# A fused attention and feed-forward kernel: the load of w_in in quarters of whole rows, batch 1's k behind it, and new orders of work for all five engines

## The chip, the cores and the metric

The kernel runs on 1 core of one Trainium2 chip. Its time is the device time of one execution in microseconds (us), as the median of several executions. The profile is of one execution, whose own time is given beside its span (the time from its first to its last instruction).

## The reference

Two stages follow one another. The first is block attention with a sorting matrix: `sort_net` (4 batches x 8 heads, each 8x8) goes through five rounds of exp and of division by row sums and by column sums (the sinkhorn steps); the result P mixes the 8 blocks of k and of v, and each block of 96 queries attends to its own mixed block of 96 keys.

```python
B, H, S, D = 4, 8, 768, 64          # 8 blocks of 96
for _ in range(5):
    P = exp(P - max(P, -1)); P = P / sum(P, -1); P = P / sum(P, -2)
k_sorted = einsum('bhij,bhjcd->bhicd', P, k_b)      # v_sorted alike
attn = softmax(q_b @ k_sb.T / 8)                    # per batch, head and block
x = (attn @ v_sb) as 3072 tokens x 512
h = x @ w_in                                        # w_in 512 x 2048
g = max(h, 0) + alpha * min(h, 0)
out = g @ w_out                                     # w_out 2048 x 512
```

## The kernel before

All work is cut into 1227 numbered operations (`G.add`, numbered in the order in which they are added). An operation is a small group of instructions on one engine or one DMA. The program does not run in the order of the numbers: the table `SEQ` lists all the numbers in one global order, and each engine takes its own operations in that order, strictly one after the other. A letter behind a number (p, a, d) chooses POOL, ACT or DVE where an operation may run on more than one engine. The waits between engines follow from what the operations read and write (`_Graph.emit`). So a table can move an operation ahead of or behind others on its engine, or to another engine, and an operation that waits holds up all that stands behind it in its engine's list. `WARM` adds matmuls on the identity whose result nobody reads (fillers, line 808): `114:9:y` puts nine of them into PE's list ahead of operation 114. `BURST` is the number of still smaller matmuls at the very start (line 888).

The attention works on groups g = 0 to 31, eight per batch. For each group: scores (line 715 in batch 0, line 712 later), their maximum on DVE (line 721), in batch 0 a second set of scores with the maximum subtracted (lines 736 and 727), exp on ACT, the product with v (line 768), the division on DVE (lines 776 and 779), and a transpose into xT (line 794 on PE, or a DMA). In batches 1 to 3 the exponentials, and q itself, are transposed by DMAs from SP's queue (ET at line 753, QTz at line 409).

Before attention, k and v of each batch are mixed: in batch 0 by matmuls at lines 600 (k) and 674 (v) after a conversion of v on POOL or DVE (line 653); later by conversions at lines 616 (k) and 658 (v), and matmuls at lines 629 and 669, with the results copied out at line 372. In batch 0 the k result also needs a pad copy (line 642) before any scores.

The feed-forward part takes tokens in chunks: the first matmul of w_in per tile of 128 features (`ffn1`, line 823), two steps on ACT (line 833) and DVE (line 836) that make hT, then `ffn2` (line 862) in four parts per 128 tokens; parts 0 and 1 read the first half of w_out, parts 2 and 3 the second.

The loads from HBM are issued by POOL into one queue (the software queue): q, k and v of batch 0 first (lines 397 and 419), then in some order k of batch 1 (419), w_in in four quarters (907), w_out in two halves (912), v of batch 1 in two halves (435) and q of batch 1 in eight pieces, one per head (401). They change f32 to bf16 on the way; the sizes in the profile are those of the bf16 result.

The operations that the texts below name by number: 4, 5, 6 the loads of q, k, v of batch 0; 130 to 133 the quarters of w_in; 134 and 135 the halves of w_out; 138 the load of k of batch 1; 147 and 148 v of batch 1; 139 to 146 q of batch 1; 403, 402 and 404 the first halves of v and the k of batch 2; 10 the memset of sel0; 72 the exp of the fifth sinkhorn round; 97 the pad copy; 158 the first scores; 196 and 193 the first two operations of ffn1; 273 the first part of the first ffn2; 361 an ffn1, 373 an ffn2 part, 383 a product with v, 388 a mixing of v; 191, 229, 235 and 238 a transpose, two ffn1 and one scores operation of batch 0; 250 a conversion of k of batch 1; 178 to 183 the transposes of q of batch 1 (QTz), of which 178 is the first; 419 the scores of group 8, the first of batch 1, which read the result of 178; 422 the ET transpose of group 8.

## Time and profile before

| | us |
|---|---|
| three executions | 238.43, 238.87, 239.08 |
| their median | 238.87 |
| the profiled execution's own time | 238.79 |
| its span | 237.1 |

| engine | busy us | share of the span | instructions |
|---|---|---|---|
| PE (matmul) | 228.4 | 96% | 2511 |
| DVE | 169.4 | 71% | 353 |
| ACT | 151.9 | 64% | 423 |
| POOL | 74.1 | 31% | 140 |

The granted TensorE clock has a mean of 1.000. The profile gives for each instruction its engine, its line in the kernel, its tiles and what it waited for. A matmul's record lasts longer than its turn on the engine, since matmuls overlap; the chain of waits shows the turns. The table of windows gives each engine's busy time in a stretch of the span, the share of the DMA engines' time taken by packets (over 1 where packets overlap) and the bytes moved.

### The profile page before, as it was taken

Reading aid. Unit: us, or ns where it says so; the run is one execution under the profiler, and the core shown is the slowest. Engines: PE = TensorE matmul, PEld = TensorE weight load, DVE = VectorE, ACT = ScalarE, POOL = GpSimd, SP = SyncE. Lnnn points to the kernel's source line nnn. Section 1 sums busy time; section 2 is a strip of 40 time slices with the busy share of each in tenths; the row PEclk is TensorE's granted clock in tenths of the full one; section 3 lists DMA queues with packets and bytes.
Section 4 is the critical chain, followed back from the end, with each engine's and each line's share of the span. In section 5 each row is a group of like instructions: output and inputs, shape, how many; then the busy total and the mean of one; then the engine's idle time right before and its main releaser. Section 6 shows DMA issues by size and latency. Waiting matters only on the chain.

```text
span 237.1 us, 6254 instructions
## 1 busy us (share of the span) xinstructions
PE 228.4 (96%) x2511; PEld 143.5 (61%) x2540; DVE 169.4 (71%) x353; ACT 151.9 (64%) x423; POOL 74.1 (31%) x140
## 2 busy tenths in 40 slices
PE   7798999999999999999999999999999999999995
PEld 3455678788666666666566665655655555555544
DVE  4745788889999997878887667676766587744350
ACT  4463356677886988886678786756863646353332
POOL 7959812905759521238292020000000000000000
PEclk9999999999999999999999999999999999999999
DMA  5999999999999998999999795542442423600033
GB/s 93 211 215 170 209 219 200 177 210 156 191 93 150 148 129 176 155 181 179 141 100 131 188 179 119 99 91 48 124 100 74 97 50 82 136 0 0 4 133 133
DMA packets 71453, 31.36 MB, mean 132 GB/s; under 512 B 64504, under 2 KB 65280, under 8 KB 71424
## 3 DMA queue, kind: packets, MB, share of 16 engines
q0 software_dynamic: 22896, 13.63, 44.0%
q1 hardware_dynamic: 48528, 17.33, 38.6%
q8 instruction: 20, 0.33, 0.6%
q14 instruction: 9, 0.07, 0.1%
HBM read 27.28 MB, written 6.29 MB: 142 GB/s over the span
## 4 chain that ended last, share of the span: by engine, by line
PE 90%; DMA 3%; DVE 3%; issue 1%; ACT 1%; POOLq 0%
PE psH L823 34%; PE psYP L862 29%; PE psS L862 4%; PE psS L712 3%; DMA hT<-in_q_dram 3%; PE psO L768 3%; PE psYP L808 3%; PE psYP L669 2%; PE psYP L629 2%; PE psS L727 2%; PE psO L794 1%; PE psS L736 1%; PE psS L715 1%; PE psO L862 1%; DVE hT L836 1%
## 5 line engine op out<-in xcount | busy, mean ns | idle before, releaser
L836 DVE SCALAR_TENSOR_TENSOR hT<-t,omaT,psH 128x384 bf16<-128x384 f32 (+1 forms) x139 | 77.3, 570 | 36.2 <-ACT t L833 34.8
L823 PE MATMUL psH<-xT,w_in_bf 128*128 128x384 bf16 (+1 forms) x556 | 96.9, 311 | 0.1
L833 ACT ACTIVATE t<-psH 128x384 f32<-128x384 f32 (+1 forms) x139 | 63.2, 462 | 49.5 <-PE psH L823 48.2
L862 PE MATMUL psYP<-w_out_bf,hT 128*128 128x512 bf16 x308 | 77.6, 379 | 1.5
L823 PEld LDWEIGHTS psH<-xT,w_in_bf 128*128 128x128 bf16 x556 | 49.5, 98 | 29.1 <-DVE hT L836 1.9
L862 PEld LDWEIGHTS psYP<-w_out_bf,hT 128*128 128x128 bf16 x336 | 30.9, 98 | 28.2
L748 ACT ACTIVATE Esb<-psS,nf 96x96 bf16<-96x96 f32 x192 | 46.3, 346 | 2.0 <-DVE nf L721 2.0
L721 DVE TENSOR_REDUCE nf<-psS 96x8 f32<-96x768 f32 x24 | 22.8, 950 | 6.5 <-PE psS L712 6.0
L658 POOL COPY VDz<-VST 64x192 f32<-64x192 f32 x39 | 20.5, 525 | 20.2 <-DMA VST<-in_v_dram 16.5
L779 DVE TENSOR_TENSOR xq<-psO,rec 96x512 bf16<-96x512 f32 x31 | 21.2, 683 | 0.5
L616 POOL COPY KSz<-KS 64x256 f32<-64x256 f32 x28 | 11.5, 412 | 32.1 <-PE psYP L629 18.8
L401 POOL DMA_DIRECT2D QN<-in_q_dram x24 | 20.0, 839 | 3.3 <-DMA QTz<-QN 2.7
L712 PEld LDWEIGHTS psS<-KT,QTz 128*96 128x96 bf16 x192 | 12.1, 124 | 3.3
L808 PE MATMUL psYP<-identb 128*128 128x512 bf16 x48 | 13.6, 419 | 0.4 <-ACT identb L372 0.4
L372 ACT ACTIVATE VS<-psYP 112x512 bf16<-112x512 f32 x15 | 10.3, 686 | 5.4 <-PE psYP L674 3.2
L768 PEld LDWEIGHTS psO<-VS,ET 112*128 112x128 bf16 x248 | 11.1, 98 | 3.6 <-ACT ET L759 0.2
L768 PE MATMUL psO<-VS,ET 112*128 112x65 bf16 x248 | 12.7, 194 | 0.0
L712 PE MATMUL psS<-KT,QTz 128*96 128x96 bf16 x192 | 12.6, 208 | 0.0
L372 ACT ACTIVATE KT<-psYP 128x512 bf16<-128x512 f32 x15 | 9.0, 599 | 2.6 <-PE psYP L629 1.6
L372 ACT ACTIVATE outstg<-psYP 128x512 f32<-128x512 f32 x13 | 7.7, 604 | 3.2 <-PE psYP L862 3.2
L669 PEld LDWEIGHTS psYP<-BDV,VDz 128*128 128x128 bf16 x192 | 8.2, 98 | 2.3 <-ACT VS L372 0.2
L669 PE MATMUL psYP<-BDV,VDz 128*128 128x64 bf16 x192 | 9.5, 193 | 0.0
(137 smaller groups left out, 200.2 us busy)
## 6 DMA issues: line engine op xcount, KB each, us to landing
out_dram<-outstg SPq DMA_DIRECT2D x23, 256.0 KB, 2.5
KS<-in_k_dram POOLq DMA_DIRECT2D x3, 768.0 KB, 13.6
QN<-in_q_dram POOLq DMA_DIRECT2D x24, 96.0 KB, 5.4
w_in_bf<-in_moe_w_in_dram POOLq DMA_DIRECT2D x4, 512.0 KB, 17.0
w_out_bf<-in_moe_w_out_dram POOLq DMA_DIRECT2D x2, 1024.0 KB, 23.6
VST<-in_v_dram POOLq DMA_DIRECT2D x4, 384.0 KB, 17.9
hT<-in_q_dram POOLq DMA_DIRECT2D x1, 768.0 KB, 7.8
VST<-in_v_dram POOLq DMA_DIRECT2D x1, 768.0 KB, 11.0
```

What stands on the lines that cost most here:

```text
L372: return e.activation(o, i, ACTF.Copy) if e is nc.scalar else e.tensor_copy(o, i)
L669: inst = e.matmul(AP(t, off + dd * 64, [[row, 128], [1, 64]]), AP(VDz, (u % VSL * 4 + dd // 2) * 256 + dd % 2, [[VSL * 1024, 128], [2, 128]]),
L712: inst = e.matmul(o, AP(QTz[n], hp * 3072 + h4 * 768 + i * 96, [[6144, 128], [1, 96]]), AP(KT[n], (h4 * 8 + i) * bk, [[ld, 128], [64, 2], ...
L721: G.add(DVE, lambda e: e.tensor_reduce(AP(nx, 0, [[8, 96], [4, 2], [1, 4]]), AP(psX, 0, [[1024, 96], [512, 2], [96, 4], [1, 96]]), AxisLis ...
L748: inst = e.activation(AP(Esb[me], p * 128, [[1024, 96], [64, 2], [1, 48]]), AP(psX, (p // 4) * 512 + (p % 4) * 96, [[1024, 96], [48, 2], [ ...
L768: inst = e.matmul(AP(psZ, hp * 512 + h4 * 68, [[1024, 128], [1, 65]]), AP(ET[me] if far else ET[m], pos(h4, hp) * 96, [[800, nk], [1, 128] ...
L779: G.add(DVE, lambda e: e.tensor_tensor(out=AP(xq[me], 0, [[512, 96], [256, 2], [64, 4], [1, 64]]), in0=AP(psZ, 0, [[1024, 96], [512, 2], [ ...
L808: inst = e.matmul(AP(bank[0], bank[1], [[1024, 128], [1, 512]]), identb[:, :], AP(identb, 0, [[128, 128], [0, 4], [1, 128]]))
L823: inst = e.matmul(AP(pt, poff, [[1024, 128], [1, n]]), AP(w_in_bf, kt * DFF + ft // 2 * 256 + ft % 2, [[KT_TILES * DFF, 128], [2, 128]]), ...
L833: G.add(ACT, lambda e: e.activation(AP(t1[tb], 0, [[384, 128], [1, n]]), AP(pt, poff, [[1024, 128], [1, n]]), ACTF.Relu, scale=-1.0), t_ac ...
L836: G.add(DVE, lambda e: e.scalar_tensor_tensor(out=AP(hT, ft * RING + tok % RING, [[FT_TILES * RING, 128], [1, n]]), in0=AP(t1[tb], 0, [[38 ...
L862: inst = e.matmul(AP(bank[0], bank[1], [[1024, 128], [1, n]]), AP(hT, ft * RING + tok % RING, [[FT_TILES * RING, 128], [1, 128]]), AP(w_ou ...
```

## The change

The four loads of w_in had taken half a row of 2048 features for two of the four blocks of 128 rows; now each takes whole rows of one block. As each first matmul of ffn1 sums over all four blocks, every ffn1 operation now waits for all four loads, where it had waited for two. `WARM`, `BURST` and `SEQ` are new; the two tables differ from their fifth number on. On POOL the loads now stand in the order 4, 5, 6, 132, 130, 133, 131, 138, then conversions of v, then 134, 147, 148, 146, 135 and the other pieces of q, with 250 ahead of the last two pieces (142 and 139). They had stood in the order 4, 5, 6, 138, 130, 131, 132, 133, 134, 147, 148, 146, 135, and so on. The operations are otherwise the same in both, with the same numbers; the fillers differ.

```diff
-BURST = 130
+BURST = 112
 WARM = """
-89:14:y 79:8:y 93:2:y 104:2:y 114:9:y 158:6:y 153:3:h 205:1:y 207:1:y 128:4:y 162:1:y
+85:10:y 79:8:y 93:1:y 104:1:y 116:6:y 158:1:y 153:2:h 196:1:y 217:1:y 291:1:i
 SEQ = """
-0 7 11 2 3 1 4 8 42 9 22 28 43 14 44 45 46 47 19 18 48 5 49 50 15 51 39 52 53 6 54 55 25 56 138 57 58 29 23 59 60
-12p 61 62 130 63 64 31 65 32 66 13 37 89 67 68 83 69 81 84 70 87 71 91 131 88 10 85 132 72 40 73 90 133 74 75 86
-134 76 41 77 82 78 26 79 92 147 80 148 93 102 94d 103a 104 95 105a 100 98 99a 38 109d 106p 35 111d 36 96a 108p 112d
-16 34 101a 33 114 107p 115d 97p 146 158 118 159 110p 116 119a 120 250p 149 121d 124 248p 160 117d 125a 113p 30 135
-136 161 122 137 150 249p 126 254p 127a 123d 24 128 144 151 129d 143 247d 17 152 162 145 163 164 153 177 253p 154
-155 20 21 165 156 166d 141 184 157a 167 185 140 168 142 169 196 193 186 194 197 195 199 198 187 27 202 170 203 205
-200 204 188 201 214 206 220 215 217 189 218 207 221 219 222 226 216 229 190 227 223 230 273 228 224 171 208 231 225
-235 191 236 238 192a 237 232 239 261 313p 251 262 209 233 347p 252a 240 210 263 139 211 255 241 270 234 403 212 264
-404 256a 213d 291 301d 271 242 258p 175 259 292 257p 274 260a 352p 265 272 267 311p 243 266 279 244 300p 293 280
-268 312p 281 282 269 310p 294 245 174 285 304d 351p 246d 275 286 283 348p 287 284 338 305p 302 339 295 303a 314 288
-296 315 306 289 316 340 307a 290 176 297 320 178 341 317 276 318 321 319 179 298 322 379 299a 308 380 323 309a 342
-326 324 343 349 344 327 381 350a 325 328 345 353 382 346d 329 354d 332 180 330 572p 383 333 331 357 277a 402 334
-335 384 361 360p 385 183 336 373 362 574p 337 358a 363 391p 419 359d 386 355p 364 420 367 573p 365 374 368 366 182
-421 356d 388 387d 370 389d 395p 375 577p 369 371 392 390p 435 372 393a 429 394p 436 396 430 376 397d 422 437 445p
...
+0 7 11 2 10 3 1 4 8 5 9 42 43 6 44 45 132 46 47 48 130 49 50 30 51 31 52 133 53 16 54 24 55 32 56 12p 57 58 40 131
+59 39 60 61 21 62 23 28 63 25 64 138 65 85 66 91 67 89 68 81 69 87 70 71 37 17 72 29 82 73 74 92 75 76 77 78 79 83
+80 84 93 94a 95 88 104 86 100 101a 98 102 103a 96a 111p 107d 90 99d 116 38 109p 105a 108d 106p 97d 110d 117a 158 20
+113d 118 114 19 159 119a 122 13 149 123a 34 124 115d 160 125d 112p 120 26 150 18 121a 136 134 128 161 137 33 147
+148 146 135 126 129d 151 127a 144 152 162 143 163 164 153 177 145 154 155 165 141 184 166d 156 185 157a 167 22 140
+196 168 193 197 169 186 41 194 198 195 199 187 170 214 250p 202 35 14 200 205 215 201 203 36 206 217 249p 188 142
+218 171 207 189 219 216 254p 226 204 208 139 223 190 220 227 238 247p 221 228 191 224 253p 222 235 239 248p 273 236
+192a 225 229 237 209 230 232 210 231 251 233 240 211 252a 261 27 234 241 212 255 213d 262 300p 291 256a 263 264
+310p 292 242 265 259 301p 270 260a 258p 266 293 271 257d 305p 243 272 311p 267 244 282 15 268 279 294 269 274 312d
+283 175 403 280 284 245 338 347p 281 246a 302 339 288 351p 303a 285 295 352p 286 306 289 296 340 287 304p 307a 290
+313p 314 297 308 348p 315 317 174 172 275 316 318 341 319 320 309d 323 321 298 379 324 322 349 299a 325 326 350a
+356p 380 329 178 342 327 353 330 328 381 354a 343 331 179 344 332 382 357 335 358d 390p 345 333 276 336 180 404 334
+337 388 355p 346d 277a 419 402 361 389a 420 364 394p 373 365 395p 362 366 421 383 363 360p 392 384 370 391p 385 374
+359p 393d 371 386 422 367 372 387a 435 368 396 432 369 397a 436 429 433 398 434 430 375 574p 437 399d 456 431 400
+453 401d 181 457 376 454 458 455 438 377a 445p 465 462 446p 466 459 578p 183 463 447d 449p 405 464 460 577p 467 461
...
@@ -825,7 +825,7 @@
                                 AP(xT, kt * XR + tok % XR, [[KT_TILES * XR, 128], [1, n]]),
                                 start=(kt == 0), stop=(kt == KT_TILES - 1))
             return inst
-        op = G.add(PE, f, t_pe(*[(n, 128)] * 4), r=[("xT", g % 16) for g in range(ga, gb)] + [("w_in", ft // 8 * 2 + x) for x in range(2)],
+        op = G.add(PE, f, t_pe(*[(n, 128)] * 4), r=[("xT", g % 16) for g in range(ga, gb)] + [("w_in", kt) for kt in range(KT_TILES)],
               w=keys, prio=prio)
         if not ffn_ops:
             ffn_ops.append(op)
@@ -905,9 +905,9 @@
         prep_v(0, u, -45, (BANK_O + [BANK_P])[u % 3])
     for p in range(4):
         G.add(POOL, lambda e, p=p: e.dma_start(
-            AP(w_in_bf, p % 2 * 2 * DFF + p // 2 * (DFF // 2), [[KT_TILES * DFF, 128], [DFF, 2], [1, DFF // 2]]),
-            AP(moe_w_in.tensor, p % 2 * 256 * DFF + p // 2 * (DFF // 2), [[DFF, 128], [128 * DFF, 2], [1, DFF // 2]])),
-            2600, w=[("w_in", p)], prio=-40 + p, dma=(dma_sem("wi%d" % p), 0))
+            AP(w_in_bf, p * DFF, [[KT_TILES * DFF, 128], [1, DFF]]),
+            AP(moe_w_in.tensor, p * 128 * DFF, [[DFF, 128], [1, DFF]])),
+            2550, w=[("w_in", p)], prio=-40 + p, dma=(dma_sem("wi%d" % p), 0))
     for p in range(2):
         G.add(POOL, lambda e, p=p: e.dma_start(
             AP(w_out_bf, p * 8 * DM, [[FT_TILES * DM, 128], [2 * DM, 4], [1, 2 * DM]]),
```

Counted from the tables: 55 fillers before (14 of them ahead of the first matmuls on q, the four of operation 177 included in the 55), 36 after (10 ahead of q). By PE's list, operation 273 is preceded before by 229 and not by 191, 235 and 238; after, by 191, 235 and 238 and not by 229. Operation 419 is preceded before by 361, 373 and 383 and not by 388; after, by 388 and not by the three. In SP's list the first transposes were 178, 179, 180, 183, 182, 422; they are 178, 179, 180, 422, 181. On POOL the load 404 stood behind 403; now eight conversions of k and v for batch 1 stand between them. Some operations change engine: 17 leave POOL and 13 come to it, and DVE has 358 instead of 353.

63 lines of the change are left out of this document (31 added, 32 removed).

## Prediction

> **What bounds the kernel now.** I read the page first, then PE's timeline from the start, then the issues of loads with their times to landing, then the chain of waits.
>
> ```profile
> span 237.1 us, 6254 instructions
> PE 228.4 (96%) x2511; PEld 143.5 (61%) x2540; DVE 169.4 (71%) x353; ACT 151.9 (64%) x423; POOL 74.1 (31%) x140
> ```
>
> PE has work in nearly all of the span, so the kernel is faster only by what PE does needlessly (fillers) or waits for. PE's timeline shows where both lie (start, duration, what; a group's duration runs a little into the next one):
>
> ```profile
> 9.14 0.44 PE L600 MATMUL psS<-identb,hT 64*64 64x64 bf16 x16 [1.58 <-DMA hT<-in_q_dram]
> ...
> 18.71 1.47 PE L808 MATMUL psYP<-identb 128*128 128x512 bf16 x6
> 20.11 0.38 PE L715 MATMUL psH<-KT,QTz 64*96 64x96 bf16 x8
> ...
> 30.77 0.83 PE L823 MATMUL psH<-xT,w_in_bf 128*128 128x192 bf16 x8
> ...
> 37.24 0.81 PE L862 MATMUL psYP<-w_out_bf,hT 128*128 128x512 bf16 x3
> ...
> 57.29 0.52 PE L712 MATMUL psS<-KT,QTz 128*96 128x96 bf16 x8
> ```
>
> Four marks: the first matmul on q at 9.14, the first ffn1 at 30.77, the first ffn2 (operation 273) at 37.24, the first scores of batch 1 (operation 419) at 57.29. Between the first mark and the third stand 41 of the 55 fillers, all but two of them ahead of the second. The chain of waits gives the turn of each kind of work (start, length, what):
>
> ```profile
> 45.42 0.33 PE psH L823 x4
> 45.75 0.17 PE psO L794 x4
> ...
> 46.25 0.86 PE psYP L862 x4
> 47.11 0.31 PE psS L715 x8
> ...
> 47.76 0.25 PE psO L768 x8
> ```
>
> A filler is a matmul of 512 columns like those of line 862, so 0.86 / 4 = 0.215 us. The other clock of the early part is the load queue. POOL's timeline gives the issues, the views of single issues the time from issue to landing:
>
> ```profile
> 7.53 0.71 POOL L907 DMA_DIRECT2D w_in_bf<-in_moe_w_in_dram  x1
> ...
> 10.09 2.12 POOL L907 DMA_DIRECT2D w_in_bf<-in_moe_w_in_dram  x3
> 12.20 0.76 POOL L912 DMA_DIRECT2D w_out_bf<-in_moe_w_out_dram  x1
> ...
> 40.78 0.82 POOL L401 DMA_DIRECT2D QN<-in_q_dram  x1
> ```
>
> ```profile
> w_in_bf<-in_moe_w_in_dram POOLq DMA_DIRECT2D x1, 512.0 KB, 16.2
> ...
> w_out_bf<-in_moe_w_out_dram POOLq DMA_DIRECT2D x1, 1024.0 KB, 23.9
> w_in_bf<-in_moe_w_in_dram POOLq DMA_DIRECT2D x1, 512.0 KB, 19.6
> ...
> QN<-in_q_dram POOLq DMA_DIRECT2D x1, 96.0 KB, 9.8
> ```
>
> So the first quarter of w_in lands at 7.53 + 16.2 = 23.7, the fourth (issued at 10.09 + 2 x 0.71 = 11.5) at 31.1, the first half of w_out at 12.20 + 23.9 = 36.1, the last piece of q of batch 1 at 40.78 + 9.8 = 50.6. They land in the order of issue, long after it. The table of windows says that the queue is full:
>
> ```profile
> 20.00:25.00 5.00, 4.23 (x132) 3.57 (x132) 2.91 (x5) 2.27 (x4) 4.34 (x10) 1.00 1.02 175
> 25.00:30.00 5.00, 4.88 (x68) 2.89 (x66) 3.75 (x10) 1.43 (x2) 4.54 (x9) 1.00 1.13 211
> ...
> 70.00:75.00 5.00, 4.87 (x54) 3.03 (x54) 4.81 (x11) 3.35 (x10) 4.88 (x8) 1.00 1.42 152
> ```
>
> After the five engines' busy times and PE's clock, the last two columns are the DMA engines' share and GB/s: the share is above 1 while the early loads run. The order of transfers can change; the bytes ahead of the last of them cannot.
>
> **The change part by part.** *The start.* The 18 matmuls that line 888 loses and the 4 fillers that go ahead of q lie before 9.14, where PE sat idle for 1.58 us until q had landed. The wait for q covers them; without that cover the four would be worth 4 x 0.215 = 0.9 us and the 18 smaller ones less. Behind q, 41 - 26 = 15 fillers fewer are 15 x 0.215 = 3.2 us, if no wait takes their place. What speaks for their going: six fillers (1.47 us) stood directly ahead of the first scores at 20.11, and now one does, so PE may begin these scores up to 5 x 0.215 = 1.1 us sooner; the pad copy that they need moves from POOL to DVE; and two steps that lay between the sinkhorn rounds (the memset 10, and copies of q ahead of the exp 72) are moved out of their way. So 1.1 of the 3.2 us have a place that the rows show, and the rest hangs on conversions and copies that are dealt out anew. Bounds: the first ffn1 starts between 30.77 (nothing of it gained) and 30.77 - 3.2 = 27.5.
>
> *The loads.* Four w_in loads directly behind v, with k of batch 1 out of their way, are all there sooner. Three quarters took 31.1 - 23.7 = 7.4 us, 2.47 each for 512 KB; k of batch 1 has 768 KB (768 / 512 x 2.47 = 3.7 us), so the last quarter lands at 31.1 - 3.7 = 27.4. Each ffn1 now waits for all four, where it waited for two; behind it on PE stands everything, so the first ffn1 cannot begin ahead of 27.4. That is no loss against 30.77. Whether whole rows move faster: a quarter is 1.05 MB of f32 read in 2.47 us, 425 GB/s; a tenth faster or slower would be 1.0 us over the four, and I take no change, since 512 KB in 2.47 us are the 211 GB/s at which the row of 25 to 30 shows the whole queue. [...] Moved to the end, k of batch 1 lands at 31.1, and POOL waits there at operation 250; behind it in POOL's list stand the last two pieces of q, which go out at some 33 and 35, while the queue is still busy with w_out and v. So that wait costs nothing.
>
> *What is late next.* The first half of w_out has the same bytes ahead of it as before, so it lands at 36.1 again. From the first ffn1 to 273 PE took 37.24 - 30.77 = 6.5 us, and its list now has 0.5 more work ahead of 273 (a scores operation 0.31, a transpose 0.17; one ffn1 replaces another) and one filler (0.2) less. From 27.5 PE is there at 34.3 and waits; from 29.4 it comes just in time. So 273 starts at about 36.2 for any first ffn1 before 29.4, and the gain at this mark is 37.24 - 36.2 + 0.5 = 1.5 us, not 3.2.
>
> *What is late after that.* Operation 419 needs the first transpose of q of batch 1, and that needs all eight pieces of q, which again land at 50.6, since again the same bytes are ahead of them. SP's timeline and the issues:
>
> ```profile
> 50.61 12.00 SPq L409 DMA_TRANSPOSE QTz<-QN  x5
> ...
> 82.74 4.05 SPq L409 DMA_TRANSPOSE QTz<-QN  x3
> ```
>
> ```profile
> QTz<-QN SPq DMA_TRANSPOSE x1, 6.1
> QTz<-QN SPq DMA_TRANSPOSE x1, 4.1
> ```
>
> The first took 6.1 us, to 56.7, while v and k of batch 2 were landing beside it; the one at 82.74 took 4.1. In the new list the load of k of batch 2 (404) goes behind eight conversions, of which the last ones wait for PE, so it leaves the transposes more room. I take 4.7 us, nearer to 4.1, with both ends kept: the transpose lands at 54.7 to 56.7, likeliest 55.3, and 419 starts at 55.45 if PE needs 0.15 to take it up. [...] When 419 starts, PE has done less than before: 361 (0.33), 373 (0.86) and 383 (0.25) are behind it, 388 (eight matmuls like those of line 768, 0.25) ahead, so 1.2 us less. The same end as before therefore asks for 419 at 57.29 - 1.2 = 56.1. PE itself would be there at 57.29 - 1.5 - 1.2, and 0.2 for the filler ahead of 291, so at 54.8. At 55.45 the gain is 56.1 - 55.45 = 0.6 us.
>
> *Behind that* both lists give PE work without a stop, as far as a reading of the lists tells. PE had 0.13 us of 5 free in the row of 70 to 75, with DVE busy for 4.81 of the 5: the new lists can gain some tenths there, or lose as much if DVE comes late at one place. I take nothing, with -0.5 and +0.8 us as ends.
>
> The sum: 238.79 (the profiled execution, span 237.1 and 1.7 around it) - 0.6 = 238.2. The profiled execution is within 0.1 of the median 238.87, so I take it for both. What this measurement can tell from no change is 0.3%, 0.7 us.
>
> **The rivals.** *The queue runs clean.* From 20 to 25 the loads moved 175 GB/s, against 211 after it; that is (211 - 175) x 5 / 211 = 0.85 us lost in the first quarter of w_in, for a reason that I don't see in the trace. If it doesn't come back, all later loads land 0.85 earlier; with the transpose at its short 4.1 us, 419 starts at 50.6 - 0.85 + 4.1 + 0.15 = 54.0, and the gain is 2.1 us: 236.7. For it: the row; against it: nothing in the change removes a cause.
>
> *All fillers saved are gained*, 3.2 us: 235.6. For it speaks that PE is the bound; against it, that w_out and q of batch 1 have the same bytes ahead of them.
>
> *Slower.* The place is operation 419, the mechanism the first transpose of q. If it takes its 6.1 us again, 419 starts at 56.7 + 0.15 = 56.9 with 1.2 us less work done ahead of it, and the kernel loses 56.9 - 56.1 = 0.8 us: 239.6. It decides from a landing later than 56.0. For it: 6.1 is what this very transpose took, and half of v of batch 2 still lands beside it. Against: k of batch 2 leaves.
>
> *The new w_in loads bring nothing.* If the chain to xT stays as late as it is and the first ffn1 comes at 30.5, PE meets w_out after 36.1 and no gate moves: 238.7.
>
> **How the numbers follow.** Forecast, 238.2 with its own ends 237.4 to 239.0: 0.42. Queue clean: 0.22. All fillers: 0.06. Slower: 0.22. Nothing: 0.08. The forecast lies at the edge of what can be told, so of its 0.42 I count 0.17 as faster and 0.25 as same. Faster: 0.17 + 0.22 + 0.06 = 0.45; same: 0.25 + 0.08 + 0.02 of the slower case = 0.35; slower: 0.20. The range goes from a little below the clean queue, 236.5, to the slower case, 239.6; the 3.2 us and larger losses behind 57 us are left out.
>
> **What would show it.** The profile after should have the first ffn1 at 27.5 to 29, a landing of all w_in by 27.5 and of w_out's first half near 36.1; line 862's first matmul at 36.2, with PE idle for up to 2 us before it and that wait put down to the DMA of w_out; the last q piece landing near 50.6, and line 712's first matmul right after the first QTz landing, at 55.45. If line 712 starts while the transpose has long landed, the gate is not the queue and the forecast's last step is wrong. If w_out lands well before 36, the clean queue is right. If PE's rows behind 60 show waits for DVE or ACT of more than 1 us, the new lists cost something that I set at nothing.

## The result, and the profile after

The changed kernel is slower. Its median is 241.92 us (four executions, 240.38 to 243.31) against 238.65 for the kernel before beside it: a ratio of 1.0138, with a 95% interval of 1.0101 to 1.0175. A second timing (e12 below) gave 241.03, ratio 1.0093 (1.0059 to 1.0127). The ratios leave out executions that took over 1.5% more than the fastest of the same kernel (one of e4 took 599.53 us); the medians keep them. The forecast was 238.2, faster, and 241.9 lies outside its range.

The profiled execution took 241.84 us, with a span of 240.1 (before: 238.79 and 237.1). The head of its page, with the row of PE's granted clock (40 equal slices of the span, 9 is full speed):

```profile
span 240.1 us, 6203 instructions
...
PE 229.6 (96%) x2503; PEld 145.1 (60%) x2503; DVE 170.8 (71%) x358; ACT 151.9 (63%) x422; POOL 72.0 (30%) x136
...
PEclk9799679999999999999999999999999999999999
```

Fewer matmuls took more PE time, and the clock, full throughout before, is low in the second slice and in the fifth and sixth. PE's timeline has the four marks of the prediction and what lies ahead of them (start, duration, what; in brackets the idle time and what ended it):

```profile
2.80 3.65 PE L808 MATMUL psYP<-identb 128*128 128x512 bf16 x10 [0.52 <-ACT identb L372]
8.88 0.63 PE L600 MATMUL psO<-identb,hT 64*64 64x64 bf16 x16 [2.42 <-DMA hT<-in_q_dram]
...
11.15 2.47 PE L808 MATMUL psYP<-identb 128*128 128x512 bf16 x8
...
19.90 0.38 PE L715 MATMUL psH<-KT,QTz 64*96 64x96 bf16 x8 [0.46 <-ACT KT L372]
...
23.42 0.32 PE L674 MATMUL psO<-BDK,hT 128*64 128x64 bf16 x8
26.45 0.85 PE L674 MATMUL psO<-BDK,hT 128*64 128x64 bf16 x24 [2.71 <-issue]
27.23 0.61 PE L736 MATMUL psS<-QTz,KT 64*112 64x96 bf16 x8
...
33.83 0.83 PE L823 MATMUL psH<-xT,w_in_bf 128*128 128x192 bf16 x8
...
40.83 1.03 PE L862 MATMUL psYP<-w_out_bf,hT 128*128 128x512 bf16 x4
...
59.28 0.54 PE L712 MATMUL psS<-KT,QTz 128*96 128x96 bf16 x8
```

The first ffn1 starts at 33.83 instead of 30.77, so 3.06 us late, and the span is 3.0 us longer: all of the loss is there by then. Two things stand out. Ahead of q PE idles for 2.42 us (1.58 before), and the matmuls behind that are slow. And in the middle of one operation, between the eighth and the ninth matmul of a group that needs nothing new, PE stops for 2.71 us "for issue", that is, for nothing that the profile shows. The table of windows gives the clock; its last three columns are PE's clock, the DMA engines' share and GB/s:

```profile
5.00:10.00 5.00, 2.58 (x48) 1.53 (x48) 3.85 (x20) 1.25 (x5) 3.23 (x10) 0.89 1.06 217
10.00:15.00 5.00, 5.00 (x97) 2.95 (x93) 1.83 (x10) 2.04 (x5) 0.00 (x0) 0.77 1.02 209
...
20.00:25.00 5.00, 3.74 (x122) 3.23 (x121) 3.96 (x10) 2.95 (x5) 4.88 (x9) 1.00 1.07 217
25.00:30.00 5.00, 3.56 (x53) 2.80 (x54) 1.44 (x3) 1.50 (x2) 4.04 (x7) 0.60 1.03 203
30.00:35.00 5.00, 5.00 (x56) 3.15 (x54) 3.22 (x9) 1.12 (x3) 4.67 (x9) 0.72 1.13 217
```

The clock is 0.89 and 0.77 behind the first gap, 0.60 and 0.72 behind the second. By the trace's record of the clock it was at half from 8.92 to 12.34 and from 25.99 to 32.82. This execution's mean clock of 0.979 is low for the kernel: the ten of e12 have 0.985 to 0.993, so the clock's share of the loss is larger here than in most. The last column says that the loads ran well: no dip to 175 GB/s from 20 to 25 this time. The issues of single loads show it too (the last of w_in issued at 6.55, the first half of w_out at 21.22, the first QTz at 48.94):

```profile
w_in_bf<-in_moe_w_in_dram POOLq DMA_DIRECT2D x1, 512.0 KB, 19.6
...
w_out_bf<-in_moe_w_out_dram POOLq DMA_DIRECT2D x1, 1024.0 KB, 14.0
...
QTz<-QN SPq DMA_TRANSPOSE x1, 5.9
```

All of w_in was there at 6.55 + 19.6 = 26.2, w_out's first half at 35.2, QTz at 48.94 + 5.9 = 54.8. Each lies ahead of the mark that it was to gate (33.83, 40.83, 59.28). The data were early, and PE came late.

### The profile page after: what moved, and what is told of

It reads as the page before. It is cut to its first block, busy times and chain, and to the rows that moved or that the text cites. A ratio compares the mean times of both kernels' runs of the same rounds, so it can differ in the third digit from the quotient of the medians.

```text
span 240.1 us, 6203 instructions
## 1 busy us (share of the span) xinstructions
PE 229.6 (96%) x2503; PEld 145.1 (60%) x2503; DVE 170.8 (71%) x358; ACT 151.9 (63%) x422; POOL 72.0 (30%) x136
## 3 DMA queue, kind: packets, MB, share of 16 engines
q1 hardware_dynamic: 48528, 17.33, 35.2%
## 4 chain that ended last, share of the span: by engine, by line
PE 88%; DMA 5%; ACT 3%; issue 2%; DVE 1%; POOLq 0%
PE psH L823 33%; PE psYP L862 29%; PE psS L862 4%; PE psS L712 3%; DMA hT<-in_q_dram 3%; PE psO L768 3%; DMA ET<-Esb 2%; PE psYP L669 2%; PE psYP L629 2%; PE psS L727 2%; PE psYP L808 1%; PE psH L808 1%; PE psS L736 1%; PE psO L794 1%; ACT KT L372 1%
## 5 line engine op out<-in xcount | busy, mean ns | idle before, releaser
L833 ACT ACTIVATE t<-psH 128x384 f32<-128x384 f32 (+1 forms) x139 | 62.4, 462 | 49.8 <-PE psH L823 48.8
L862 PE MATMUL psYP<-w_out_bf,hT 128*128 128x512 bf16 x336 | 83.3, 379 | 0.0
L616 POOL COPY KSz<-KS 64x256 f32<-64x256 f32 x27 | 10.8, 399 | 38.5 <-PE psYP L629 33.4
L372 ACT ACTIVATE VS<-psYP 112x512 bf16<-112x512 f32 x14 | 9.7, 689 | 3.8 <-PE psYP L669 3.0
L372 ACT ACTIVATE outstg<-psYP 128x512 f32<-128x512 f32 x14 | 8.3, 600 | 3.6 <-PE psYP L862 3.4
L808 PE MATMUL psYP<-identb 128*128 128x512 bf16 x29 | 9.5, 459 | 0.5 <-ACT identb L372 0.5
L862 PE MATMUL psS<-w_out_bf,hT 128*128 128x512 bf16 (+1 forms) x48 | 9.6, 344 | 0.0
```

The lines of the kernel that those rows point to most:

```text
L372: return e.activation(o, i, ACTF.Copy) if e is nc.scalar else e.tensor_copy(o, i)
L833: G.add(ACT, lambda e: e.activation(AP(t1[tb], 0, [[384, 128], [1, n]]), AP(pt, poff, [[1024, 128], [1, n]]), ACTF.Relu, scale=-1.0), t_ac ...
L862: inst = e.matmul(AP(bank[0], bank[1], [[1024, 128], [1, n]]), AP(hT, ft * RING + tok % RING, [[FT_TILES * RING, 128], [1, 128]]), AP(w_ou ...
```

## The experiments

**Theory A.** PE's start sets the time. Fillers that look like waste keep PE busy where it would wait (in the change's trace the clock is at half from 8.92 us on, behind the gap of 2.42), and they also slow PE's way through its own instructions, which by this theory arrive in blocks of 256 by DMA, behind the loads (the trace of before lists 20 packets of 16 KB in one instruction queue; e2 counts the 256, e8 tests the loads). **Rival B**: the loads of w_in or their new order delay the first ffn1. **Rival C**: the new lists of the engines are worse as such. All ratios below are to the kernel before, run beside each kernel, with 95% intervals. The runs are spread over four chips (e1 to e4, e5 to e8, e9 to e16, e17 and e18), so across these groups ratios are compared, not times.

**e1, four fillers back ahead of q.**

```diff
-85:10:y 79:8:y 93:1:y 104:1:y 116:6:y 158:1:y 153:2:h 196:1:y 217:1:y 291:1:i
+85:14:y 79:8:y 93:1:y 104:1:y 116:6:y 158:1:y 153:2:h 196:1:y 217:1:y 291:1:i
```

> The changed kernel with 14 fillers ahead of q's first matmul instead of 10 (four more matmuls of 512 columns, 0.9 us, inside a wait of 2.42 us). Theory A (PE's idle time drops the clock, and PE is fed its instructions too slowly in a second place): the granted clock stays full from 8.9 to 12.3 us, where it was half; the eight fillers behind it take 1.90 us again instead of 2.47; the stop of 2.7 us in the middle of line 674's matmuls moves or shrinks, but need not go. The time falls by 0 to 1.5 us against 241.9. Rival B (the first ffn1 waits for data of w_in) and rival C (the new lists of ACT, DVE and POOL are worse): no change, within 0.7 us of 241.9, and the first ffn1 at 33.8 again.

240.04 us, ratio 1.006 (1.0026 to 1.0094), so by the ratios 0.8 to 1.9 us faster than the change (1.0093 and 1.0138) with four more matmuls; the interval overlaps that of the change's second timing. PE's timeline:

```profile
8.79 0.44 PE L600 MATMUL psO<-identb,hT 64*64 64x64 bf16 x16 [0.43 <-DMA hT<-in_q_dram]
...
10.17 1.90 PE L808 MATMUL psYP<-identb 128*128 128x512 bf16 x8
...
24.64 0.94 PE L674 MATMUL psO<-BDK,hT 128*64 128x64 bf16 x28 [2.36 <-issue]
...
30.73 0.83 PE L823 MATMUL psH<-xT,w_in_bf 128*128 128x192 bf16 x8
```

The gap ahead of q is 0.43, the eight fillers behind it take 1.90 again instead of 2.47, and the first ffn1 comes at 30.73. Not all of the smaller gap is the four fillers: at the start a filler takes 0.42 us until the clock first goes to full, which was at 7.63 in this trace and at 5.51 in the change's. The second stop is still there. The direction is what A expected, and neither B nor C; by itself the run doesn't decide.

**e2, fewer small matmuls at the start**, which moves only the count of PE's instructions.

```diff
-BURST = 112
+BURST = 62
```

> The changed kernel with 50 fewer small matmuls at the very start (100 fewer instructions in PE's list, all ahead of q). They end long before q lands, so no work behind q changes; only the places at which every 256th PE instruction falls move, by 100 instructions. Theory A (the stop of 2.7 us is PE waiting for the next 256 of its instructions): the stop leaves its place at line 674 and turns up 100 instructions later, or shrinks; the time moves by 1 to 3 us either way. Rivals B (data of w_in) and C (the lists): no change, 241.9 within 0.7, first ffn1 at 33.8.

240.06 us, ratio 1.0065 (1.0029 to 1.0102). The stop left its place. This kernel's timeline has it within another group, and a small one further ahead:

```profile
14.47 0.37 PE L600 MATMUL psH<-BDK,KS 64*64 64x64 bf16 x11 [0.28 <-issue]
...
20.64 0.54 PE L674 MATMUL psO<-BDK,hT 128*64 128x64 bf16 x12 [1.39 <-issue]
```

Numbered through the trace (matmuls, weight loads and PE's own semaphore instructions), PE stops behind number 961 in the changed kernel, behind 705 (0.51 us) and 961 in e1, behind 449 and 705 here: each is 193 plus a multiple of 256. Matmuls whose result nobody reads had moved the stop, so it belongs to the instruction count. The time went the way of A, though part of it is q, which landed earlier in this execution (8.31).

**e3, twelve fillers more, ahead of the first scores.**

```diff
-85:10:y 79:8:y 93:1:y 104:1:y 116:6:y 158:1:y 153:2:h 196:1:y 217:1:y 291:1:i
+85:10:y 79:8:y 93:1:y 104:1:y 116:6:y 158:13:y 153:2:h 196:1:y 217:1:y 291:1:i
```

> The changed kernel with 13 fillers instead of one ahead of the first scores (operation 158): 12 x 0.215 = 2.6 us of needless work added. Theory A (PE runs out of instructions there and the idle time halves its clock): the fillers lie where PE would have stood idle, the stop at line 674 falls below 1 us, the clock stays full from 26 to 33 us, the first ffn1 comes at 31 to 32.5 instead of 33.8, and the kernel gets faster by 1 to 2.5 us in spite of the added work. Rivals B (data of w_in) and C (the lists): the same or slower by up to 2.6 us.

239.92 us, ratio 1.004 (0.9997 to 1.0084): 2.6 us of needless work, and by the ratios 1.3 to 2.3 us faster than the change, though the interval overlaps that of its second timing. Its PE timeline:

```profile
24.48 0.22 PE L674 MATMUL psO<-BDK,hT 128*64 128x64 bf16 x2 [0.17 <-issue]
...
25.86 0.41 PE L736 MATMUL psS<-QTz,KT 64*112 64x96 bf16 x8
...
30.33 0.83 PE L823 MATMUL psH<-xT,w_in_bf 128*128 128x192 bf16 x8
```

The stop is 0.17 there (another of 0.66 comes one block earlier, at 18.00), and from the scores of line 736 to the first ffn1 PE needs 30.33 - 25.86 = 4.5 us, where the change needed 33.83 - 27.23 = 6.6 at half clock. So of the second place's cost in the change's profile some 2.5 us are the stop and 2.1 the clock behind it. Ahead of q this trace was lucky: q landed early enough to leave a gap of 1.18 us, and the clock stayed full with ten fillers.

**e4, whole rows alone**, in the kernel before, with each ffn1 waiting for all four loads, lists unchanged.

```diff
-... [("w_in", ft // 8 * 2 + x) for x in range(2)],
+... [("w_in", kt) for kt in range(KT_TILES)],
-            AP(w_in_bf, p % 2 * 2 * DFF + p // 2 * (DFF // 2), [[KT_TILES * DFF, 128], [DFF, 2], [1, DFF // 2]]),
+            AP(w_in_bf, p * DFF, [[KT_TILES * DFF, 128], [1, DFF]]),
```

> The kernel before with only the loads of w_in changed: whole rows, and each ffn1 waiting for all four. All lists and fillers are those of before. Theory A: the four land by about 31, the first ffn1 comes at 30.8 to 31.3, and the time is that of before within 0.7 us (238.7). Rival B (waiting for all four, or the whole rows themselves, cost the time): first ffn1 at 32 or later and slower by 1.5 us or more.

238.18 us, ratio 0.9969 (0.9929 to 1.0009), first ffn1 at 30.23. The new form of the loads costs nothing. The part of B that blames it falls.

**e5, the change's few fillers in the old lists** (one fewer than in the change, which has one ahead of 291).

```diff
-BURST = 130
+BURST = 112
-89:14:y 79:8:y 93:2:y 104:2:y 114:9:y 158:6:y 153:3:h 205:1:y 207:1:y 128:4:y 162:1:y
+89:10:y 79:8:y 93:1:y 104:1:y 114:6:y 158:1:y 153:2:h 205:1:y 207:1:y
```

> The kernel before (its lists and its loads) with the change's number of fillers only: 10 instead of 14 ahead of q, 16 fewer behind it, and the change's 112 small matmuls at the start. No step of ACT, DVE or POOL is moved and no load. Theory A (missing fillers leave PE idle, which drops its clock, and let it outrun its instruction supply): slower than before, by 1 to 3.5 us (239.5 to 242), with a granted clock of 0.978 to 0.993, and a stop put down to nothing at every 256th instruction ahead of the first ffn1. Rivals B (loads) and C (lists): faster by up to 1 us or the same, since only needless work is gone.

240.41 us, ratio 1.0064 (1.0025 to 1.0102): with nothing done but needless work taken away, the kernel is slower by 1.6 us. Its timeline has the same stop at the same line, and all ten executions have a mean clock of 0.979 to 0.986 (most of the kernel before beside it have 1.0):

```profile
24.81 0.86 PE L674 MATMUL psO<-BDK,hT 128*64 128x64 bf16 x25 [2.88 <-issue]
```

**e6, the old number of fillers in the new lists.**

```diff
-BURST = 112
+BURST = 130
-85:10:y 79:8:y 93:1:y 104:1:y 116:6:y 158:1:y 153:2:h 196:1:y 217:1:y 291:1:i
+85:14:y 79:8:y 93:2:y 104:2:y 116:9:y 158:6:y 153:3:h 196:1:y 217:1:y 128:4:y 162:1:y
```

> The changed kernel (its lists and its loads) with as many fillers as before, 51 instead of 32, and 130 small matmuls: 4.1 us of needless work put back, 0.9 of it ahead of q. Theory A: the clock stays full, the stop at line 674 falls below 1 us, the first ffn1 comes at 30.5 to 31.8, and the time is 238.4 to 240.0, 2 to 3.5 us faster than the change as it stands. Rival C (the lists): 241.9 or slower.

239.3 us, ratio 1.0006 (0.9975 to 1.0037), a clock of 0.999 or 1.0 in all ten, first ffn1 at 30.21. With e5 this is the cross of lists and fillers: old lists slow down by 0.64% when fillers go, new lists by 0.9 to 1.3% (1.0093 and 1.0138 against 1.0006); with many fillers the two lists can't be told apart. C falls as the main cause, and with it what is left of B, since e6 has the new loads and their order too.

**e7, only the four fillers ahead of q taken from the kernel before** (89:14 becomes 89:10).

> The kernel before with only the four fillers ahead of q's first matmul taken away (10 instead of 14), in a wait of 1.6 us, which grows to 2.4. My prediction set this at nothing. Theory A: the clock goes to half for one stretch of 3.4 us at some 9 to 12 us in those executions in which q lands late enough (a mean clock of 0.993 instead of 1.0), and these are slower by 0.5 to 1.5 us; the median lies 0 to 1.2 us above 238.4. Rivals B and C: no change within 0.3 us.

238.86 us, ratio 1.002 (0.9975 to 1.0064): the median shows nothing. The spread does. Eight of ten executions had a clock of 0.993 or 0.986, and the three at 0.986 took 241.2 to 241.4. So the first gap alone costs little in the median, and the larger part is behind q.

**e8, the w_in loads and k of batch 1 moved back in POOL's list**, to directly ahead of 134, so that the load queue runs empty.

```diff
-0 7 11 2 10 3 1 4 8 5 9 42 43 6 44 45 132 46 47 48 130 49 50 30 51 31 52 133 53 16 54 24 55 32 56 12p 57 58 40 131
+0 7 11 2 10 3 1 4 8 5 9 42 43 6 44 45 46 47 48 49 50 30 51 31 52 53 16 54 24 55 32 56 12p 57 58 40
...
-113d 118 114 19 159 119a 122 13 149 123a 34 124 115d 160 125d 112p 120 26 150 18 121a 136 134 128 161 137 33 147
+113d 118 114 19 159 119a 122 13 149 123a 34 124 115d 160 125d 112p 120 26 150 18 121a 136 132 130 133 131 138 134 128 161 137 33 147
```

> The changed kernel with its four w_in loads and k of batch 1 moved in POOL's list from about 3.5 to 8 us to directly ahead of w_out (about 21 us), so that the load queue runs empty from about 16 us until then. Theory A (PE's instructions come late because they are fetched through the same DMA engines behind these loads): the fetches follow their places within some 2 us instead of 4 to 5, and the stop of 2.7 us at line 674 goes below 0.5 us, with no clock drop from 26 us on. The first ffn1 comes much later, at 33 to 37, because w_in itself now lands that late, so the time is no better than 241.9. If the stop stays at 2 us or more at the same place with an empty queue, the loads are not its cause and that half of theory A falls.

Slower, 246.18 us in the profiled execution and 255.55 in the only other, since w_in itself came late (PE waited 5.80 us for it at 34.55). What it was for is the stop. Its lines stand 16 higher (690 is 674). The table of windows and PE's timeline:

```profile
15.00:20.00 5.00, 4.44 (x111) 2.66 (x104) 3.11 (x5) 4.81 (x10) 3.62 (x6) 1.00 0.03 6
20.00:25.00 5.00, 4.92 (x158) 4.31 (x155) 4.41 (x11) 3.33 (x6) 4.88 (x10) 1.00 0.53 86
```

```profile
22.51 0.45 PE L690 MATMUL psO<-BDK,hT 128*64 128x64 bf16 x16
...
23.22 0.98 PE L690 MATMUL psO<-BDK,hT 128*64 128x64 bf16 x32
24.13 0.41 PE L752 MATMUL psS<-QTz,KT 64*112 64x96 bf16 x8
```

With the DMA engines idle from 15 to 20 us (share 0.03, 6 GB/s; the moved loads start at 21.04) the group that had been torn apart by 2.71 us runs whole, 32 matmuls from 23.22, with the same few fillers. A gap of 0.3 us in it lies between its two operations, 17 instructions behind the edge of the block. The clock is full from 12.31 to 32.79. So in this trace it is the loads that had kept the instructions back. The trace lists the packets of the instruction queue, 16 KB each. Their starts, beside PE's way through its blocks (the stop is counted here from the start of the last matmul ahead of it, so it is 0.2 to 0.4 us more than the idle time of the timeline):

```
kernel    PE enters a block   packet for the next starts   PE enters the next   stop
before          16.07                  21.08                     23.45          0.98
after           18.86                  24.02                     26.44          2.90
e1              17.95                  22.16                     24.63          2.55
e5              17.34                  22.43                     24.81          3.07
e10             20.77                  24.97                     27.36          2.00
e17             22.30                  28.04                     30.50          1.23
e8              18.67                  18.05                     23.34          none
```

In all six that stop, PE goes on 2.37 to 2.47 us after the packet starts. The packet starts 4.2 to 5.7 us after PE has entered the block before, and in e8, with an empty queue, it had started already. So in these rows a block of 256 instructions takes 6.6 us or more from one entry to the next. The changed kernel's PE was through it in 23.54 - 18.86 = 4.7 us and stood for the rest. It is no fixed floor: the block before this one took the changed kernel 4.9 us (13.9 to 18.86) and ended without a stop, beside loads as well, for the packet of the next one started at 16.14, only 2.2 us after the entry.

**e9, a mixture that was to beat both.**

```diff
-BURST = 112
+BURST = 62
-85:10:y 79:8:y 93:1:y 104:1:y 116:6:y 158:1:y 153:2:h 196:1:y 217:1:y 291:1:i
+85:14:y 79:8:y 93:1:y 104:1:y 116:6:y 158:7:y 153:2:h 196:1:y 217:1:y 291:1:i
```

> The changed kernel with 14 fillers ahead of q, 7 instead of one ahead of the first scores, and 62 instead of 112 small matmuls at the start (which moves the 256-instruction boundaries by 100). Theory A: no clock drop ahead of q, the stop at a boundary shrinks to some 0.5 us, the first ffn1 comes at 28.5 to 30.5. But as the earlier variants of the changed lists gave back about 1 us of what they had won at the first ffn1 in waits for w_out, QTz and ET, the time is 237.3 to 239.0, near that of before (238.6). Rival C (the lists): 241 or more.

A miss: 241.54 us, ratio 1.0095 (1.0063 to 1.0127).

**e10, e6 with its boundaries moved** (BURST 130 becomes 66).

> The changed kernel with as many fillers as before, and 66 instead of 130 small matmuls at the start: all boundaries of 256 PE instructions move by 128, so that the first ffn1 lies in the middle of a block and not just behind a boundary (there PE had stopped for 0.6 us). Theory A: the stop ahead of the first ffn1 goes, another of up to 1 us may come up in the middle of a block near 20 or 26 us; the time is that of the same kernel with 130 (239.3) within 0.8 us. If the boundaries didn't matter, no stop would move at all.

A miss in the size: 241.65 us, ratio 1.0101 (1.0057 to 1.0146), 2.3 us slower than e6 for 64 small matmuls fewer. Its timeline:

```profile
14.50 0.25 PE L600 MATMUL psH<-BDK,KS 64*64 64x64 bf16 x3 [0.81 <-issue]
...
27.36 0.31 PE L736 MATMUL psS<-QTz,KT 64*112 64x96 bf16 x5 [1.78 <-issue]
```

The stops moved as expected, and grew. The traces of both misses have this in common: with 112 or 130 small matmuls PE passes instruction 193 at 1.95 us, and the next packet starts at 4.5 to 5.1; with 62 and 66 it passes 193 only when q has landed (9.1 and 8.6), and that packet starts at 12.1 or 12.2. The small matmuls at the start thus draw one block of instructions in early. That this is the reason for both misses is likely and not shown: e2 has its packet at 12.1 too, and wasn't slower than the change.

**e11, the whole load part of the change in the old lists** (whole rows, and 138 behind 133).

> The kernel before with the whole load part of the change and nothing else: w_in by whole rows, each ffn1 waiting for all four, and k of batch 1 issued behind w_in instead of ahead of it. Lists of all engines and fillers are those of before otherwise. Theory A (PE's start sets the time, not the loads): 238.6 within 0.7 us, w_in landed by 28, first ffn1 at 30 to 31. Rival B (the loads cost the time): slower by 1.5 us or more. If the loads were the bound that my prediction took them for: faster by 0.5 us or more.

A miss: 246.67 us, ratio 1.0309 (1.026 to 1.0359). POOL's timeline and PE's say why (its lines stand 10 higher):

```profile
30.03 0.86 POOL L626 COPY KSz<-KS 64x256 f32<-64x256 f32 x2 [9.81 <-DMA KS<-in_k_dram]
30.95 0.51 POOL L663 COPY hT<-VST 128x192 f32<-128x192 f32 x1
```

```profile
31.60 0.64 PE L684 MATMUL psO<-BDK,hT 128*64 128x64 bf16 x16 [6.46 <-POOL hT L663]
```

In the old list conversions of k (250, 248) stand ahead of a conversion of v that PE needs. With k loaded last, POOL waits 9.81 us for it and PE 6.46 for v. The change avoids this by moving those conversions too. So the load order needs lists that fit it; in the change's own trace POOL waits for k only 0.96 us.

**e12, the change as it stands, again.**

> The changed kernel as it stands, timed again beside the others on one chip. Expected 241 to 243 us, with a mean granted clock of 0.979 to 0.993 in nearly all executions and the stop of 2 to 3 us at line 674 in its profile. If it came out near 239, the difference to the other kernels would be one of the chip and not of the fillers.

241.03 us, as told above, all ten executions at a clock of 0.985 to 0.993. This profile has a lucky start, with the first ffn1 at 31.01, and still a span of 238.9. The rest went in another place:

```profile
86.77 0.40 PE L768 MATMUL psO<-VS,ET 112*128 112x65 bf16 x8 [1.84 <-DMA ET<-Esb]
```

A second cause, then, which the profile shown first hardly has (the transpose issued at 83.05 took 4.8 us there, and PE waited 0.3 for it). In these traces, whose clock is full from the first ffn1 on, the wait accounts for what differs between them behind the first ffn1:

```
kernel   first ffn1   span    from ffn1 to end   PE's waits for ET   without them
after      33.83      240.1        206.3               0.3              206.0
e12        31.01      238.9        207.9               1.8              206.1
e1         30.73      238.1        207.4               1.4              206.0
e3         30.33      237.2        206.9               0.6              206.3
e6         30.21      237.2        207.0               0.8              206.2
```

In these traces the late ET transpose lies beside the eight loads of q of batch 2, which the new list sends out in one bunch (in e1 from 74.3 to 81.7 us; before, spread from 68.9 to 80.1). In e1 it took 6.0 us from its issue at 79.93 to landing, where the shortest of that trace takes 2.8.

**e13, e14, e15: four of these loads earlier** (415, 413, 418 and 411 to directly ahead of 479p), in e6, in the change, and in e3.

```diff
-451 182 573p 423 479p 406 424 425 475p 483 452d 480p 468 426 176 486 450p 484 448d 427a 476p 485 495 278 487 477
+451 182 573p 423 415 413 418 411 479p 406 424 425 475p 483 452d 480p 468 426 176 486 450p 484 448d 427a 476p 485 495 278 487 477
```

> The changed kernel with as many fillers as before (which took 239.3, ratio 1.0006), and four of the eight loads of q of batch 2 (operations 415, 413, 418, 411) issued at about 68 to 71 us, ahead of conversions of v, instead of at 74 to 77. If the bunch of these loads is what delays the ET transposes: the waits of 0.4 us for ET at 80 and 104 us go, and the kernel is 0.3 to 0.9 us faster, at or slightly below the time before (ratio 0.996 to 1.000). If it isn't: no change, or slower by the conversions that now come later.

> The change as it stands (241.0 and 241.9 in two timings) with the same four loads issued earlier. Bunch theory: executions in which the start lost little no longer wait 1.9 us for ET near 86 us, the lowest falls below 239.5 and the median to 239.8 to 241; the stop near 24 us and the clock drop behind it stay. Otherwise: 241 to 242 again.

> The changed kernel with 13 fillers ahead of the first scores (239.92, ratio 1.004) and the same four loads issued earlier. Bunch theory: the wait of 0.6 us for ET at 80 us goes, and the time falls to 238.3 to 239.5. Otherwise 239.9 again.

All three missed: 242.63 (ratio 1.0147, 1.0101 to 1.0193), 246.45 (1.0314, 1.0269 to 1.0358) and 244.61 us (1.0224, 1.0171 to 1.0277). POOL had to wait for the transposes of batch 1 before it could overwrite QN, and the conversions queued behind that wait came late for PE. In e13:

```profile
70.29 3.33 POOL L407 DMA_DIRECT2D QN<-in_q_dram  x4 [3.44 <-DMA QTz<-QN]
```

```profile
75.98 0.39 PE L675 MATMUL psYP<-BDV,VDz 128*128 128x64 bf16 x8 [3.73 <-POOL VDz L664]
```

They say nothing of the bunch, since they put another wait in its place.

**e16, the converse: the bunch in the kernel before** (415, 413, 418, 411, 412, 414 and 417 moved behind 510p).

> The kernel before, with its loads of q of batch 2 issued behind the conversions 479 to 510 of v and in one bunch, as the change does it, and nothing else changed. Bunch theory: one or two ET transposes near 80 to 87 us land 4 to 6 us after their issue, PE waits 0.5 to 2 us for them in line 768, and the kernel is slower by 0.3 to 1.5 us. Otherwise: no change.

242.53 us, ratio 1.0118 (1.0079 to 1.0157), slower, but not where it was expected. ET waits total 0.2 us, and PE waits 2.75 us at 109 for a conversion of v. Again another wait, so the time says nothing. One half of the theory is in the trace, though: beside the bunch the ET transposes issued at 76.23 and 81.14 took 5.5 and 5.2 us to land, where their like in the kernel before (76.04 and 80.95) took 4.4 and 3.1.

**e17 and e18: four of the loads later** (412, 414, 417 and 416 behind 535p), so that the conversions come no later, in e6 and in e1.

```diff
-... 412 472 519 473d 505d 571p 522 512d 414 ...
+... 472 519 473d 505d 571p 522 512d ...
-... 524 537 416 543 ...
+... 524 537 543 ...
-... 572p 540a 535p 502 551 ...
+... 572p 540a 535p 412 414 417 416 502 551 ...
```

> The changed kernel with as many fillers as before (239.3, ratio 1.0006; waits for ET of 0.39 us at 80 and 0.42 us at 104), and the last four loads of q of batch 2 (412, 414, 417, 416) issued behind the conversions 536, 572 and 535 instead of ahead of them. Bunch theory: the ET transpose issued at 79.4 lands within 4 us instead of 5.4, the wait at 80 us (and one near 85 us, where there is one) goes, and the time falls by 0.3 to 0.8 us. Otherwise no change, within 0.3 us.

> The changed kernel with 14 fillers ahead of q (240.04, ratio 1.006; its profile had a wait for ET of 1.4 us at 86) and the same four loads issued later. Bunch theory: the wait of 1.4 us at 86 falls below 0.4 us and the time to 238.8 to 239.6. Otherwise 240.0 within 0.4, with the wait still there.

e17: 238.9 us, ratio 0.9987 (0.9957 to 1.0017), waits for ET 0.5 in all instead of 0.8; within its interval of e6. e18: 239.23 us, ratio 0.9997 (0.9964 to 1.0031) against 1.006 (1.0026 to 1.0094) for e1. The ET transpose issued at 80.98 landed 4.0 us later, and no wait is left. The view of ET's transposes from 70 to 92 us, of e12 first and then of e18:

```profile
who waited for it (us, times):
  PE psO L768: 1.8, 1
...
DMA to landing us min/median/max: 2.8/3.3/6.4
```

```profile
who waited for it (us, times):
...
DMA to landing us min/median/max: 2.8/3.4/4.2
```

From the first ffn1 (31.77) to the end e18 needs 237.8 - 31.77 = 206.0 us, the same as the last column above. So the late ET transpose is the second cause in these traces, and the bunch is what most likely makes it late: e18 against e1 and the landings of e16 speak for it, e17 can't tell. e18's start still has a stop of 2.08 us and a clock of 0.986 to 0.993: it reaches the time before with the first cause half in place. No version here is faster than the kernel before beyond its interval; the nearest are e4 and e17.

## Why the prediction was wrong, point by point

**"The wait for q covers them."** This is the step that failed first. I costed the four fillers and the 18 small matmuls by their length and put them in PE's idle time, as if idle time were free. It isn't: with 2.42 us idle ahead of q the clock was at half from 8.92 to 12.34, with 1.58 before it wasn't. Chance has a part in it: e12, the same kernel again, idles for 1.76 us there and keeps its clock, and so does e6 with 2.04, split over two of the windows told of below. I had the row with the 1.58 on the page and asked what it hid, and not what it did. Alone this costs little in the median (e7), 1 to 2 us together with the rest (e1).

**"Behind q ... 15 fillers fewer are 15 x 0.215 = 3.2 us, if no wait takes their place."** One did, and this step carries the larger part. The new wait was for instructions: 2.71 us behind number 961, and 2.1 us more through the half clock behind it. The bounds that I drew for the first ffn1, 27.5 to 30.77, had no way to be late, because I took "nothing gained" as the worst case of removing work. It came at 33.83. The old kernel's trace had a sign of it, a stop of 0.8 us "for issue" behind the same instruction number:

```profile
23.45 0.46 PE L727 MATMUL psH<-identb,nm 96*112 96x96 bf16 x6 [0.77 <-issue]
```

Against before, the longer stop (2.7 - 0.8 = 1.9), the half clock behind it (2.1) and the slower stretch from q to the matmul of line 539 (13.55 - 8.88 against 12.64 - 9.14, so 1.2) make 5.2 us; less the 3.2 of the fillers that is 2.0, where 3.06 were lost. The other 1.1 lies for the most part between line 539 and the first scores. Ten of the 15 fillers went there, 2.15 us, and the stretch became only 1.12 us shorter (20.11 - 12.64 = 7.47 before, 19.90 - 13.55 = 6.35 after): PE now waits 0.46 us for KT in it, and does 16 matmuls on q (at 13.85) that had stood ahead of line 539.

**The loads** were read rightly, and better than forecast: w_in whole at 26.2 (27.4), w_out at 35.2 (36.1), QTz at 54.8 (54.7 to 56.7). QTz's time is partly luck: its q was there 1.7 us sooner than forecast (first issue at 48.94, not 50.6), and the transpose took 5.9 us and not 4.7. In other traces of the new lists it took 3.3 (e1), 3.4 (e12) and 4.2 (e18). The prediction's 425 GB/s count f32 as read; the 211 GB/s of its table of windows count the bf16 that was written (512 KB in 2.47 us). The dip of 20 to 25 us didn't come back, which was the rival "the queue runs clean". That waiting for all four quarters costs nothing was right (e4, first ffn1 at 30.23 and no wait for w_in). All this decided nothing, since PE reached each gate 4 to 8 us after the data.

**Operation 419** was to start right behind QTz. It started 4.4 us later, at 59.28, which the prediction named as the sign that the gate is not the queue. Against the start that would have given the same end (56.1) it was 3.2 us late, and the execution was 3.05 us longer: that part of the sum held.

**"Behind that both lists give PE work without a stop"**: in the first profile it looks right (206.3 us from the first ffn1 to the end in both kernels). In other traces of the new lists the ET wait, a term set at nothing, takes 0.6 to 1.8 us (e1, e3, e6, e12), and none in e18.

**The slower rival** had the right sign and the wrong place. QTz landed in 5.9 us, close to its 6.1, and did no harm.

## What to carry to other kernels

Before taking fillers away, ask what each keeps going: the clock across the next wait (here 2.42 us idle ahead of q, then half clock), and the distance between PE and its instructions while loads fill the DMA queues (here a stop of 2.71 us behind number 961, and none in e8, whose loads came later); a gap "for issue" inside one operation, at a fixed count of instructions (here 193 plus a multiple of 256), was the sign of the second. Removing work is bounded by zero only if nothing was paced by it, so draw the range to the slow side too. When a first cause is mended, look at the same trace again further down, and when a transfer is moved within a queue, move what waits for it on the same engine as well (e11, e13).

## What the runs showed of the hardware that was not expected

**The clock.** It changes on a grid of 3.41 us: in the change's trace at 5.51, 8.92, 12.34, 25.99 and 32.82 us, which are one, one, four and two steps of 3.41. Counted over the 20 traces of these kernels, with PE's idle time (between the records of its matmuls) in each such window while the clock was full: of 18 windows with 1.9 us idle or more, all were followed by half clock; of 22 with 1.1 to 1.9, five were; of 1287 with less, two. So the idle time need not fill a window: the gap of 2.42 us in the change's trace was followed by half clock from 8.92 to 12.34, the one of 2.36 in e1 by a mean clock of 0.69 from 25 to 30 us. The grid starts elsewhere in each execution (full clock first at 5.51 us in the change's trace, at 5.99, 7.63 and 4.59 in those of before, e1 and e6), so the same gap can fall into one window or be split over two. That would explain why the same kernel loses its clock in one execution and not in the next: in the timing beside e5, 17 executions of the kernel before had a clock of 0.999 or 1.0 and took 238.07 to 239.30, eight had 0.993 and took 239.65 to 240.73.

**Instructions.** The stops lie behind numbers 449, 705, 961 and 1217 of PE's list, 256 apart, and in the table under e8 one packet of 16 KB starts ahead of each entry into the next block. If each packet brings 256 instructions, an estimate from these two, the 20 packets in the trace of before bring 5120; PE has 2511 matmuls and 2540 weight loads there, 5051 in all. A crossing cost up to 2.88 us of idle time (e5). One packet of 16 KB took 0.97 us in the change's trace, beside load packets of 4 and 6 KB that took 0.32 and 0.47 us each.

**Left open.** Why half clock lasts one window in some cases (8.92 to 12.34 in the change's trace) and two (25.99 to 32.82 there) or three (e2, whose mean clock of 0.978 over a span of 238.9 us means some 10 us at half) in others was not tried, nor whether smaller or differently spread loads would let the instruction packets through sooner; e4, with w_in packets of 4 KB instead of 2 KB, shows little difference (packets at 20.03 and 26.51, 4.5 and 3.9 us after PE entered a block; before, at 21.08 and 27.29, 5.0 and 3.8 us). Why a packet starts 2.2 us after PE enters one block and 5.2 after the next is open too, and the bunch of q loads as the reason for the late transpose rests on one pair of runs.
